# Where the next group's rows are turned, in a fused attention, Fourier mixing and expert kernel: six edits of order

## The chip, the cores and the metric

The kernel runs on one core of one Trainium2 chip. The metric is device microseconds of one execution. Three runs of the kernel before took 918.91, 921.63 and 917.93 us, so their median is 918.91 us. The profiled execution took 917.5 us, of which its trace spans 915.7 us.

Five engines run at the same time, each through a list of instructions in its own order: TensorE (PE in the rows, its weight loads PEld), VectorE (DVE), ScalarE (ACT), GpSimd (POOL) and SyncE (SP), which here only issues DMAs. An instruction that waits for another engine holds up what stands behind it in its own list.

## The reference, cut to what matters

Three layers follow each other, for 4 batches of 576 tokens with 512 features:

```python
# 1. attention, 8 heads of 64, window of 128, causal, a linear bias per head
attn = softmax(where(mask, scale * q @ k.T + bias, -1e9));  x = attn @ v     # (B, S, 512)
# 2. Fourier mixing, then a two-layer product on normalised rows
u  = x + real(fft(fft(x, axis=1), axis=2))
un = (u - mean(u)) / sqrt(var(u) + 1e-6)
x2 = u + maximum(un @ w_ch1, 0) @ w_ch2                                      # hidden width 2048
# 3. one expert of 8 per token; some tokens keep the expert of the token before
logits = x2 @ w_gate;   keep = sigmoid(x2 @ w_local) >= 0.5
out[s] = softmax(logits[s])[e] * (maximum(x2[s] @ w1[e], 0) @ w2[e])         # e chosen token by token
```

## The kernel before

**Tiles and precision.** The 2304 tokens are 18 tiles of 128 rows. Nine groups of two tiles go through layer 2. Large products are made of three TensorE products on numbers split in a high and a low part (`mm3`: high weights times high input, high weights times low input, low weights times high input). `split` makes the parts: ScalarE copies the high part, VectorE subtracts it from the source to get the low part.

**A pass of layer 2.** The hidden width is done in two halves. `mlp_first` runs the first half for the nine groups while attention and mixing of later batches still go on; the second half runs after all of them. A pass of `ffn` over one group has eight hidden blocks. Block f takes 12 products into the tile `hps` (lines 184 to 186), ScalarE takes the maximum with zero (line 732), VectorE makes its low part (line 735), and then 6 products add block f-1 into `acc` (lines 754 and 758). `ffn` yields after each of these pieces: piece 0 is block 0's `hps`, piece 2f-1 is block f's `hps`, piece 2f is `acc` of block f-1, piece 15 the last `acc`. So pieces 11 and 13 are the `hps` of blocks 6 and 7, and pieces 12, 14 and 15 the `acc` of blocks 5, 6 and 7.

**Preparation of the next group.** Between the pieces of group j, `normalise` prepares group j+1 one step at a time, behind the pieces that the table `STEPS` names: ask for the rows (0), statistics (3), the reciprocal root on GpSimd (5), scaling of both tiles on ScalarE into `u` (10, line 875), then `transpose_split` of each tile (13 and 15): four TensorE transposes into `tps` (line 704), a ScalarE cast into the high part of `xT` (line 180), a VectorE subtraction into its low part (line 181), and a store of `xT` for the second half (line 880, SyncE). Group j+1's first product reads the high part of both tiles, its second one the low part. Where the rows are not mixed yet, the preparation begins later, at piece 5 or when they are. After a pass, ScalarE copies both `acc` tiles out and stores them (lines 916 and 917). Group 0 has its own table, `STEPS0`.

**Attention.** `attention` takes the ten units of a batch through four parts: `scores` and a row minimum, `exps` on ScalarE, `flip` (four transposes, tile `pt`, and the mask on GpSimd), `values` (products into `o`, copied to `ot`, lines 459 to 467), and `natural` (transposes of `ot` into `xps`, line 479, then a reciprocal and a product on VectorE into `x`). Units are staggered: in step u the parts work on units u, u-1, u-2, u-3 and u-4. From batch 1 on, a step yields twice, and `natural` of unit u-4 stands at the head of the step.

**What sets the order.** The opening (batch 0 and the first normalisation) is written out by hand. After it, `run` picks the next piece from lanes (attention, mixing, layer 2, weight conversion) by their due positions, and a scheduler sets each engine's order from there. PSUM tiles of the small parts (`pt`, `o`, `xps`, `tps`, `zps`) share three buffers.

**The router.** In the second half, `route` makes the logits of a group with eight products of 256 columns (line 1220): for each of the four feature blocks, one with the high part of `x2T` and one with its low part.

Of the kernel before, what the change touches and what calls it, by code (L numbers as in the profile page):

```python
# [65 lines left out]
VL = 3  # L66
NP = 5

STEPS = (0, 3, 5, 10, 13, 15)
STEPS0 = (9, 11, 12, 13, 14, 15)  # L70

QK = 2 * (HALF + 33)
# [100 lines left out]
def build(ctx, tc, a, out):  # L173
# [161 lines left out]
    def load_part(b, g, part):  # L335

        t = qk.tile([P, 2, QK], F32, tag="qk", name="qkt")
        nc.sync.dma_start(out=t, in_=a["qk"][b, g, part])
        return t, load_values(b, g, part)
# [50 lines left out]
    def attention(b, between=None):  # L390
# [103 lines left out]
        for u in range(len(units) + VL + 1):  # L494
            if ahead < 4 and u in (0, 2, 5):
                g, p = parts[ahead]
                R[g, p] = load_part(b, g, p)
                ahead += 1
            if b == 1 and u == 6:
                three = slab([P, 2, K1 + 1], F32, "three", "m", MB)  # L500
                nc.sync.dma_start(out=three, in_=a["three"])
            if b == 1 and u == 10:
                nc.scalar.copy(tab3, three)
                nc.gpsimd.tensor_tensor(out=tab3[32:64], in0=three[32:64], in1=tab3[32:64].bitcast(F32), op=ALU.subtract)
            if u < len(units) and b == 0:
                scores(u)
            if b == 0 and u == FL:
                flip(0)
            if 1 <= u < len(units) + 1:
                exps(u - 1)  # L510
            if b:
                if VL < u:
                    natural(u - VL - 1)
                if FL <= u < len(units) + FL:
                    flip(u - FL)
                yield
                if u < len(units):
                    scores(u)
                if VL <= u < len(units) + VL:
                    values(u - VL)  # L520
                yield
                continue
            yield

            def fill():
                if b == 0 and u >= len(units) - 1:
                    spin(SPIN_)

            def back():
                if VL < u:  # L530
                    natural(u - VL - 1)

            def weights():
                if FL <= u < len(units) + FL:
                    if b or u > FL:
                        flip(u - FL)
                    fill()

            def mean():
                if VL <= u < len(units) + VL:  # L540
                    values(u - VL)
                    fill()

            part = (back, weights, mean)
            if b == 0:
                part = {len(units): (mean, weights, back), len(units) + 1: (back, weights, between, mean), len(units) + 2: (mean, back)}.get(u, part)
            for p in part:
                p()
            yield
# [264 lines left out]
    def normalise(gs, xT, j, src=None):  # L814
        n = len(gs)
        mv = sm2.tile([P, TM, 2], F32, tag="mv", name="mv")
        st = sm2.tile([P, TM, 6], F32, tag="st", name="st")
        later = src is None
        if later:
            if j not in rows_of:  # L820
                ask_rows(j)
            src = rows_of[j]
        yield
        for i in range(n):
            nc.vector.bn_stats(st[:, i], src[i])
            if i + 1 < n and not later:
                yield
        for i in range(n):
            nc.vector.bn_aggr(mv[:, i], st[:, i])
        yield  # L830

        v = sm2.tile([P, 3, TM], F32, tag="v", name="v")
        v0, v1, v2 = (v[:, i, 0:n] for i in range(3))

        eng = nc.gpsimd if later else nc.vector
        eng.tensor_scalar_add(v0, mv[:, 0:n, 1], 1.0e-6)
        if later:
            nc.gpsimd.tensor_tensor(out=v1, in0=v0, in1=half[:, 0:n], op=ALU.pow)
            for _ in range(2):
                eng.tensor_tensor(out=v2, in0=v1, in1=v1, op=ALU.mult)  # L840
                eng.tensor_tensor(out=v2, in0=v2, in1=v0, op=ALU.mult)
                eng.tensor_scalar(out=v2, in0=v2, scalar1=-0.5, scalar2=1.5, op0=ALU.mult, op1=ALU.add)
                eng.tensor_tensor(out=v1, in0=v2, in1=v1, op=ALU.mult)
            eng.tensor_tensor(out=v2, in0=mv[:, 0:n, 0], in1=v1, op=ALU.mult)
            eng.tensor_scalar_mul(v2, v2, -1.0)
        else:

            nc.gpsimd.tensor_tensor(out=v1, in0=v0, in1=half[:, 0:n], op=ALU.pow)
            eng.tensor_scalar_mul(v0, v0, -0.5)
            for _ in range(2):  # L850
                eng.tensor_tensor(out=v2, in0=v1, in1=v1, op=ALU.mult)
                eng.tensor_tensor(out=v2, in0=v2, in1=v0, op=ALU.mult)
                eng.scalar_tensor_tensor(out=v1, in0=v2, scalar=1.5, in1=v1, op0=ALU.add, op1=ALU.mult)
            last["v"] = eng.scalar_tensor_tensor(out=v2, in0=mv[:, 0:n, 0], scalar=-1.0, in1=v1, op0=ALU.mult, op1=ALU.mult)
        yield
        if not later:
            us = []
            for i in range(n):
                us.append(act.tile([P, DM], F32, tag="u", name="u", bufs=UB))
                if i:  # L860
                    nc.vector.tensor_scalar(out=us[i], in0=src[i], scalar1=v[:, 1, i:i + 1], scalar2=v[:, 2, i:i + 1], op0=ALU.mult, op1=ALU.add)
                else:
                    nc.scalar.activation(us[i], src[i], AF.Identity, scale=v[:, 1, i:i + 1], bias=v[:, 2, i:i + 1])
            yield
            for i, g in enumerate(gs):
                transpose_split(xT, i * P, us[i])
            for i, g in enumerate(gs):
                nc.sync.dma_start(out=nd[g], in_=xT[:, :, :, i * P:(i + 1) * P].bitcast(F32))
            yield
            return  # L870
        us = []
        with behind():
            for i in range(n):
                us.append(act.tile([P, DM], F32, tag="u", name="u", bufs=UB))
                nc.scalar.activation(us[i], src[i], AF.Identity, scale=v[:, 1, i:i + 1], bias=v[:, 2, i:i + 1])
        yield
        for i, g in enumerate(gs):
            with behind():
                transpose_split(xT, i * P, us[i])
            nc.sync.dma_start(out=nd[g], in_=xT[:, :, :, i * P:(i + 1) * P].bitcast(F32))  # L880
            yield
# [9 lines left out]
    def prepare(j, src=None):  # L891
        xT = act.tile([P, 2, 4, TM * P], F32R, tag="xT", name="xT")
        ph[j] = xT
        return normalise(GA[j], xT, j, src)

    def mlp_first():

        need = [0, 0, 1, 1, 2, 2, 3, 3, 3]
        for j, gs in enumerate(GA):
            xT = ph.pop(j)  # L900
            acc = []
            pre = None
            done = 0
            steps = STEPS if j else STEPS0
            for n, _ in enumerate(ffn(xT, len(gs) * P, chunksA, banks, acc, hidden, (ps_a, ps_a))):
                if j + 1 < len(GA) and done < len(steps) and n >= steps[done]:
                    if pre is None and (n >= NP or mixed[0] >= need[j + 1]):
                        yield ("need", lambda: mixed[0] >= need[j + 1])
                        pre = prepare(j + 1)
                    if pre is not None:  # L910
                        next(pre)
                        done += 1
                yield ("piece", 1)
            for i, g in enumerate(gs):
                y = act.tile([P, DM], F32, tag="y", name="y")
                nc.scalar.copy(y, acc[i])
                nc.scalar.dma_start(out=pd[g], in_=y)
            if pre is not None:
                for _ in pre:
                    yield ("piece", 0)  # L920
# [292 lines left out]
    def route(gs, xT, apart, late_copy):  # L1213
        n = len(gs) * P
        ng = len(gs)
        ps = ps_g.tile([P, DM], F32, tag="g", name="lps")
        r2 = 2 * (E + 2)
        for k in range(4):
            for j in range(2):
                nc.tensor.matmul(ps[0:r2, 0:n], lhsT=wg[:, k].rearrange("p h e -> p (h e)"), rhs=xT[:, j, k, 0:n],  # L1220
                                 start=k == 0 and j == 0, stop=k == 3 and j == 1)
        lt = lact.tile([r2, TM * P], F32, tag="lt", name="lt", bufs=1)
# [462 lines left out]
    with tc.If(most > 0):  # L1685
        for r in range(E):
            n = nc.values_load(eid[0:1, 3, r:r + 1], min_val=0, max_val=-(-(NT - CAPS[r]) // P))
# [54 lines left out]
```

## Time and profile before

| | |
|---|---|
| median of three runs | 918.91 us (917.93 to 921.63) |
| profiled execution | 917.5 us, trace 915.7 us |
| TensorE busy | 877.0 us, 96% of the span |
| VectorE, ScalarE, GpSimd busy | 527.5, 385.0 and 220.4 us |
| first halves of the nine groups | about 62 to 416 us of the span |
| mean granted clock of TensorE | 0.991 |

Starts are counted from the trace's first instruction. A row of the timeline gives start and length in us, engine, source line, operation, tile written, tiles read, shape and how many equal instructions follow each other; in brackets stands how long the engine was idle before it and which engine and line ended that. A TensorE instruction counts as busy while it is in the pipe, so that the next one starts before it ends.

### The profile page before, as it was taken

How to read it: one execution, taken by the hardware profiler on the slowest of the kernel's cores; microseconds unless marked ns; L12 is line 12 of the kernel's file. 1: busy time of each engine (PE TensorE's matmuls, PEld its weight loads, DVE VectorE, ACT ScalarE, POOL GpSimd, SP SyncE). 2: the span in 40 equal slices, each digit the busy share in tenths (PEclk: the TensorE clock that was granted, in tenths of full speed). 3: DMA queues.
4: the chain of work that ended last, by engine and by line, in shares of the span. 5: the costliest groups of instructions: out<-in, count | busy, mean ns of one | idle time of the engine just before them, and what ended most of it. 6: DMA issues, size and time to landing. Idle time of an engine off the chain costs nothing. (4 is left out here: it accounts for less than half of the span.)

```text
span 915.7 us, 16165 instructions
## 1 busy us (share of the span) xinstructions
PE 877.0 (96%) x5919; PEld 740.9 (81%) x5919; DVE 527.5 (58%) x1360; ACT 385.0 (42%) x1012; POOL 220.4 (24%) x351
## 2 busy tenths in 40 slices
PE   8987999999999999999999999999999999999993
PEld 5665777778788889889888898888888889888882
DVE  6889957785766687111334535366955655556410
ACT  5756664654553364211122121114534655545311
POOL 2433421431321331010111322223130321122100
PEclk9998999999999999999999999999999999999997
DMA  9942432451405881263444552347735765455100
GB/s 325 384 160 64 152 131 70 146 155 42 151 2 161 259 273 51 69 161 70 116 115 115 104 113 42 102 103 214 217 97 184 255 215 176 153 184 180 69 21 22
DMA packets 103743, 128.75 MB, mean 141 GB/s; under 512 B 10704, under 2 KB 72400, under 8 KB 103622
## 3 DMA queue, kind: packets, MB, share of 16 engines
q1 hardware_dynamic: 78246, 103.54, 34.9%
q0 software_dynamic: 22720, 19.36, 9.5%
q10 hardware_dynamic: 2688, 4.73, 1.4%
q8 instruction: 49, 0.80, 0.3%
q14 instruction: 40, 0.33, 0.1%
HBM read 99.24 MB, written 30.19 MB: 141 GB/s over the span
## 5 line engine op out<-in xcount | busy, mean ns | idle before, releaser
L754 PE MATMUL acc<-t,h 128*128 128x512 f32 x608 | 175.2, 406 | 1.0 <-ACT t L180 1.0
L732 ACT ACTIVATE h<-hps 128x256 fp32r<-128x256 f32 x152 | 58.3, 383 | 267.6 <-PE hps L186 266.8
L735 DVE SCALAR_TENSOR_TENSOR h<-hps,h 128x256 fp32r<-128x256 f32 x152 | 63.8, 420 | 137.3 <-ACT h L732 135.9
L754 PEld LDWEIGHTS acc<-t,h 128*128 128x128 f32 x608 | 105.3, 190 | 19.2 <-issue 1.9
L181 DVE TENSOR_TENSOR t<-we,t 128x512 fp32r<-128x512 f32 x128 | 84.2, 687 | 36.7 <-ACT t L180 34.0
L758 PE MATMUL acc<-t,h 128*128 128x512 f32 x304 | 95.6, 396 | 0.4 <-DVE h L735 0.4
L184 PE MATMUL hps<-xT,t 128*128 128x256 f32 x288 | 84.4, 295 | 5.6 <-ACT xT L180 3.5
L180 ACT CAST t<-we 128x512 fp32r<-128x512 f32 x128 | 74.3, 618 | 27.1 <-PE acc L758 22.1
L185 PE MATMUL hps<-xT,t 128*128 128x256 f32 x288 | 82.6, 287 | 1.5 <-DVE xT L181 1.5
L184 PE MATMUL hps<-xTb,t 128*128 128x256 f32 x288 | 83.9, 291 | 0.0
L184 PE MATMUL hps<-xTe,t 128*128 128x256 f32 (+6 forms) x288 | 83.5, 290 | 0.0
L185 PE MATMUL hps<-xTe,t 128*128 128x256 f32 (+6 forms) x288 | 83.0, 288 | 0.0
L186 PE MATMUL hps<-xTe,t 128*128 128x256 f32 (+6 forms) x288 | 82.9, 288 | 0.0
L186 PE MATMUL hps<-xT,t 128*128 128x256 f32 x288 | 82.1, 286 | 0.0
L186 PE MATMUL hps<-xTb,t 128*128 128x256 f32 x288 | 81.4, 283 | 0.0
L185 PE MATMUL hps<-xTb,t 128*128 128x256 f32 x288 | 81.4, 283 | 0.0
L431 ACT ACTIVATE t<-t,mx 128x128 f32<-128x128 f32 (+1 forms) x160 | 62.4, 392 | 29.0 <-DVE mx L424 25.8
L754 PE MATMUL acc<-t,hE 128*128 128x512 f32 (+3 forms) x256 | 70.9, 399 | 0.3 <-ACT hE L732 0.3
L758 PEld LDWEIGHTS acc<-t,h 128*128 128x128 f32 x304 | 56.8, 189 | 13.8 <-DVE h L735 1.1
L184 PEld LDWEIGHTS hps<-xT,t 128*128 128x128 f32 x288 | 55.0, 192 | 12.2 <-ACT xT L180 4.6
L735 DVE SCALAR_TENSOR_TENSOR hE<-hps,hE 128x256 fp32r<-128x256 f32 (+3 forms) x96 | 29.7, 338 | 59.9 <-ACT hE L732 57.8
L185 PEld LDWEIGHTS hps<-xT,t 128*128 128x128 f32 x288 | 55.4, 192 | 4.1 <-DVE xT L181 2.3
(327 smaller groups left out, 1857.2 us busy)
## 6 DMA issues: line engine op xcount, KB each, us to landing
we<-in_w SPq DMA_DIRECT2D x64, 512.0 KB
rw<-in_w_ch SPq DMA_DIRECT2D x32, 512.0 KB
qkt<-in_qk SPq DMA_DIRECT2D x15, 642.0 KB
nd<-xT SPq DMA_DIRECT2D x18, 512.0 KB
xTb<-nd POOLq DMA_DIRECT2D x18, 512.0 KB
vt<-in_v SPq DMA_DIRECT2D x16, 384.0 KB
pd<-y ACTq DMA_DIRECT2D x18, 256.0 KB
ub<-ud SPq DMA_DIRECT2D x18, 256.0 KB
```

The source lines that it names most:

```text
L180: last["hi"] = nc.scalar.copy(hi, src)
L181: return (eng or nc.vector).tensor_tensor(out=lo, in0=src, in1=hi.bitcast(F32), op=ALU.subtract)
L184: nc.tensor.matmul(o, lhsT=wh, rhs=xh, start=start, stop=False, **kw)
L185: nc.tensor.matmul(o, lhsT=wh, rhs=xl, start=False, stop=False, **kw)
L186: return nc.tensor.matmul(o, lhsT=wl, rhs=xh, start=False, stop=stop, **kw)
L431: nc.scalar.activation(t[0:m, j], t[0:m, j], AF.Exp, bias=mx[0:m, j:j + 1], scale=-1.0, accum_out=sums[0:m, j:j + 1])
L732: last["relu"] = nc.scalar.activation(h[:, 0:n], hps[:, 0:n], AF.Relu)
L735: last["rest"] = nc.vector.scalar_tensor_tensor(out=h[:, lo:lo + c1 - c0], in0=hps[:, c0:c1], scalar=0.0, in1=h[:, c0:c1].bitcast(F32), op ...
L754: nc.tensor.matmul(acc[t][0:m], lhsT=h[:, c:c + m], rhs=t2[:, j, g % per], start=g == 0 and j == 0, stop=False)
L758: last["acc"] = nc.tensor.matmul(o, lhsT=x, rhs=t2[:, j, g % per], start=first_ and j == 0, stop=g == nf - 1 and j == js[-1])
```

## The change

There are six edits of order; the number of instructions of each kind stays the same. Transposes of the next group's rows stand behind pieces 11 and 13 instead of 13 and 15. Where the preparation began late, a new table puts them behind 13 and 14. In batches 1 to 3, `natural` goes from the head of a step to its end. In the opening, VectorE scales tile 0 and ScalarE tile 1 instead of the other way round. In the router, all four products with high parts stand ahead of the four with low parts.

```diff
-STEPS = (0, 3, 5, 10, 13, 15)
+STEPS = (0, 3, 5, 10, 11, 13)
+LATE = (0, 3, 5, 10, 13, 14)
 STEPS0 = (9, 11, 12, 13, 14, 15)
...
             if b:
-                if VL < u:
-                    natural(u - VL - 1)
                 if FL <= u < len(units) + FL:
                     flip(u - FL)
                 yield
...
                 if VL <= u < len(units) + VL:
                     values(u - VL)
+                if VL < u:
+                    natural(u - VL - 1)
                 yield
...
-                if i:
+                if not i:
                     nc.vector.tensor_scalar(out=us[i], in0=src[i], ...)
                 else:
                     nc.scalar.activation(us[i], src[i], AF.Identity, ...)
...
                         pre = prepare(j + 1)
+                        if j and n > 0:
+                            steps = LATE
...
-        for k in range(4):
-            for j in range(2):
+        for j in range(2):
+            for k in range(4):
                 nc.tensor.matmul(ps[0:r2, 0:n], lhsT=wg[:, k]..., rhs=xT[:, j, k, 0:n], ...)
```

In the orders below, a row is source line, operation, tile written, tiles read, shape and count. Line numbers of the changed file are one to three higher than before for the same statement (704 is 705, 916 is 919).

TensorE before, at the end of the first half of group 7, before group 8 begins; `t_1173` and `t_787` are weights of the last and first hidden blocks, `t_1257` the second layer's for the last two:

```order
L186 MATMUL hps<-xT,t_1173 128x256
L704 MATMUL tps<-ident,u 128x128 x4
L754 MATMUL acc<-t_1257,h 128x512 x4
L758 MATMUL acc<-t_1257,h 128x512 x2
L754 MATMUL acc<-t_1257,h 128x512 x4
L758 MATMUL acc<-t_1257,h 128x512 x2
L704 MATMUL tps<-ident,u 128x128 x4
L184 MATMUL hps<-xT,t_787 128x256 x2
L185 MATMUL hps<-xT,t_787 128x256
```

TensorE of the changed kernel at the same place:

```order
L187 MATMUL hps<-xT,t_1173 128x256
L705 MATMUL tps<-ident,u 128x128 x4
L755 MATMUL acc<-t_1257,h 128x512 x4
L759 MATMUL acc<-t_1257,h 128x512 x2
L755 MATMUL acc<-t_1257,h 128x512 x4
L759 MATMUL acc<-t_1257,h 128x512 x2
L185 MATMUL hps<-xT,t_787 128x256
L186 MATMUL hps<-xT,t_787 128x256
```

Tile 1's transposes moved from behind the two last `acc` pieces to ahead of them; tile 0's, which stood there, moved up by one block (they stand behind block 6's `hps`, 15 rows further up).

ScalarE before, over the same pass; `u` are the scaled rows, `h` the hidden block, `y` the `acc` copies:

```order
L875 ACTIVATE u<-r,v 128x512 x2
L732 ACTIVATE h<-hps 128x256 x2
L180 CAST xT<-tps 128x4x128
L916 COPY y<-acc 128x512
L180 CAST xT<-tps 128x4x128
L917 DMA pd_92<-y 128x512
L916 COPY y<-acc 128x512
```

ScalarE of the changed kernel over the same pass:

```order
L876 ACTIVATE u<-r,v 128x512 x2
L733 ACTIVATE h<-hps 128x256
L181 CAST xT<-tps 128x4x128
L733 ACTIVATE h<-hps 128x256
L181 CAST xT<-tps 128x4x128
L919 COPY y<-acc 128x512 x2
```

Tile 1's cast stood behind the first copy of the finished pass, and now stands right behind the last hidden block, with tile 0's cast ahead of that block.

TensorE before, in batch 2's attention beside the first half of group 1 (about 182 to 186 us of the trace):

```order
L459 MATMUL o<-w,vt 64x128 x7
L754 MATMUL acc<-t_1112,h 128x512 x4
L758 MATMUL acc<-t_1112,h 128x512 x2
L479 MATMUL xps<-ident,ot 128x128 x2
L440 MATMUL pt<-ident,t 128x128 x4
```

TensorE of the changed kernel at that place:

```order
L460 MATMUL o<-w,vt 64x128 x8
L480 MATMUL xps<-ident,ot 128x128 x2
L755 MATMUL acc<-t_1112,h 128x512 x4
L759 MATMUL acc<-t_1112,h 128x512 x2
L441 MATMUL pt<-ident,t 128x128 x4
```

The two transposes of `ot` before take the unit whose `o` products stand right above them; in the changed kernel they take the unit before that one.

## Rows read from the trace of the kernel before

**Rows 1.** Busy time by stretch: stretch, its length, engines' busy us, granted clock, DMA

```profile
60.00:105.00 45.00, 38.85 (x247) 28.62 (x248) 43.81 (x77) 28.62 (x82) 14.43 (x15) 0.92 0.37 117
76.00:83.00 7.00, 6.36 (x21) 4.87 (x21) 7.00 (x15) 3.64 (x10) 1.82 (x2) 0.51 0.08 20
105.00:312.00 207.00, 202.52 (x1564) 164.50 (x1563) 143.31 (x347) 107.10 (x357) 57.99 (x147) 1.00 0.36 115
312.00:417.00 105.00, 100.05 (x633) 89.14 (x633) 53.19 (x107) 43.10 (x88) 21.16 (x33) 1.00 0.50 154
```

**Rows 2.** Waits of TensorE, whole span: waited for, us in total, times, longest

```profile
PE hps L184 <- ACT xT L180: 3.5, 4, 1.2
PE pt L440 <- ACT t L431: 3.3, 4, 1.2
PE xps L479 <- ACT ot L467: 1.6, 2, 1.2
...
PE hps L185 <- DVE xT L181: 1.5, 4, 0.8
...
PE tps L704 <- ACT u L863: 0.8, 1, 0.8
...
PE lps L1220 <- DVE x2T L181: 0.7, 1, 0.7
```

**Rows 3.** Timeline, TensorE, from group 4's pass to group 5's

```profile
312.07 0.60 PE L704 MATMUL tps<-ident,u 128*128 128x128 f32 x4
312.43 1.18 PE L754 MATMUL acc<-t,h 128*128 128x512 f32 x4
...
315.27 0.60 PE L704 MATMUL tps<-ident,u 128*128 128x128 f32 x4
317.06 0.50 PE L184 MATMUL hps<-xT,t 128*128 128x256 f32 x2 [1.19 <-ACT xT L180]
...
317.79 0.39 PE L185 MATMUL hps<-xT,t 128*128 128x256 f32 x1 [0.22 <-DVE xT L181]
```

**Rows 4.** Timeline, TensorE, from group 5's pass to group 6's

```profile
340.88 0.49 PE L704 MATMUL tps<-ident,u 128*128 128x128 f32 x3
342.21 0.51 PE L184 MATMUL hps<-xT,t 128*128 128x256 f32 x2 [0.84 <-ACT xT L180]
...
343.51 0.38 PE L185 MATMUL hps<-xT,t 128*128 128x256 f32 x1 [0.79 <-DVE xT L181]
```

**Rows 5.** Timeline, all engines, from group 7's pass to group 8's

```profile
388.56 2.09 POOL L1531 DMA_DIRECT2D xTb<-nd  x2 [42.33 <-PE hps L186]
...
389.33 0.69 DVE L181 TENSOR_TENSOR xT<-tps,xT 128x512 fp32r<-128x512 f32 x1 [0.21 <-ACT xT L180]
...
391.27 0.60 PE L704 MATMUL tps<-ident,u 128*128 128x128 f32 x4
391.47 0.59 ACT L916 COPY y<-acc 128x512 f32<-128x512 f32 x1 [2.17 <-PE acc L758]
...
391.95 0.59 ACT L180 CAST xT<-tps 128x512 fp32r<-128x512 f32 x1
...
392.60 0.50 PE L184 MATMUL hps<-xT,t 128*128 128x256 f32 x2 [0.73 <-ACT xT L180]
...
393.32 0.39 PE L185 MATMUL hps<-xT,t 128*128 128x256 f32 x1 [0.22 <-DVE xT L181]
```

**Rows 6.** Timeline, ScalarE and TensorE, in batch 2's attention

```profile
184.78 0.36 ACT L465 COPY ot<-o 128x256 f32<-128x256 f32 x1
...
185.19 0.44 PE L479 MATMUL xps<-ident,ot 128*128 128x128 f32 x2 [0.90 <-ACT ot L465]
```

**Rows 7.** Timeline, ScalarE, VectorE and TensorE, in the opening's normalisation

```profile
59.03 0.81 ACT L863 ACTIVATE u<-x,v 128x512 f32<-128x512 f32 x1 [0.47 <-DVE v L854]
...
59.03 0.55 DVE L861 TENSOR_SCALAR u<-x,v 128x512 f32<-128x512 f32 x1
...
59.90 1.09 PE L704 MATMUL tps<-ident,u 128*128 128x128 f32 x8 [0.78 <-ACT u L863]
```

## The prediction
> **What bounds the kernel now.** I read the views in this order: busy time by stretch, TensorE's waits, then the timeline at the longest of them.
>
> The table by stretch shows who sets the time where the change acts [rows 1]. From 312 to 417 us, when attention and mixing are over and layer 2's first half runs alone, TensorE is busy 100.05 of 105 us, so only its own 4.95 us of waits can be taken from it. From 105 to 312 us it idles 4.5 of 207 us; of the other engines VectorE works most, 143 us. From 60 to 105 us the picture differs: VectorE is busy 43.8 of 45 us with the weight conversion and TensorE 38.9. There a reordering of TensorE's list gains little, because what it waits for is late anyway.
>
> The waits say what the 4.95 us are [rows 2]. The first product of a pass waits 3.5 us in 4 cases for the high part of `xT`, and the second kind of product 1.5 us in 4 cases for its low part: 5.0 us, four of each. The timeline shows that these are the four last changes of group [rows 3 to 5] (the one from group 6 to 7 repeats the pattern of the last). The earlier ones show no such wait, since attention and mixing have products to put in between.
>
> What happens at such a change is seen best at the last one [rows 5]. Tile 1's transposes start at 391.27, as the last thing of the pass. ScalarE then first takes up a copy of the finished `acc` (391.47), then the cast (391.95); TensorE starts the new pass at 392.60 and stops again until VectorE has made the low part (393.32). The chain is transposes, cast, subtraction, and nothing lies beside it.
>
> **The change part by part.**
>
> *Row transposes.* Nothing is added or removed: 8 transposes, 2 casts, 2 subtractions and 2 stores per group are issued earlier. I price the wait at the four changes by starts. Where nothing is late, the product behind four transposes starts 0.36 us after the first of them (312.07 to 312.43) [rows 3]. Where the chain ends last it starts 1.79 us after it (315.27 to 317.06) [rows 3], and 1.33 us after it in the three others (340.88 to 342.21, 391.27 to 392.60) [rows 4, 5]. That is 1.43 + 3 x 0.97 = 4.3 us. The second stop adds the 1.5 us of idle time for the low parts [rows 2]. Together 5.8 us.
>
> Does the new place hide the chain? The row that shows it is in the same trace: tile 0's transposes stand, before the change, exactly where tile 1's stand after it, behind block 7's `hps`. From there to the end of the last `acc` piece it is 3.2 us (312.07 to 315.27) [rows 3]. In the last such pass tile 0's low part was done at 389.33 + 0.69 = 390.0, 1.2 us before that end at 391.27 [rows 5]. Tile 0 itself moves up by one block more. What is late next is a plain hidden block. ScalarE's cast now stands ahead of block 7's maximum, but tile 0's cast did not hold up `acc` where it stood. The two copies of `acc` (0.59 us each) now come right at the end of the pass; the next writer of `acc` comes only after two `hps` blocks. Bounds: 5.0 us, the idle time alone [rows 2], and 7.8 us, if the whole of the restart between first and third product (0.73 + 1.30 + 2 x 0.72 = 3.5 us) went [rows 3 to 5]. I take 5.8, nearest to the starts that rows show.
>
> The Trainium skill (Perfetto Trace Analysis, "Tensor Engine Instruction (MATMUL, LD_WEIGHTS)") says that the end of a TensorE instruction in the profile is estimated, not observed. By that, the idle column understates a stop and starts are the safer measure; by the idle column this term would be 5.0, and by starts it is what I took.
>
> The stores of `xT` pass other loads on SyncE's list, and on GpSimd's list one addition for the second half now stands ahead of the load that was issued at 388.56 [rows 5]. The loaded tile is needed when the next pass is over, and a pass takes 25.1 us (317.06 to 342.21) [rows 3, 4]; a delay of a few us there is covered, so I price it at nothing.
>
> *Attended rows last.* Before, the transposes of a unit's result stand right behind the products that make it, with ScalarE's copy in between: at 185.19 TensorE has stood for 0.90 us because the copy ran from 184.78, behind that unit's exponentials [rows 6]. In the changed order a unit's flip, scores and the next unit's values lie between. These waits are 1.6 us (copy of line 467) and 0.90 us [rows 2, 6], 2.5 us at most. The change only moves where in a step TensorE meets ScalarE, and other waits may come instead; the nearest row is the flip's wait for exponentials, 3.3 us in 4 cases [rows 2]. So this term lies between +2.5 and -3.3. I take 1.5, because in the new order the distance grows for every unit, while nothing else in a step gets closer.
>
> *First rows on VectorE.* Both engines start scaling at 59.03; ScalarE takes 0.81 us, VectorE 0.55, and the transposes of tile 0 wait for ScalarE's tile [rows 7]. After the swap tile 0 is ready 0.26 us earlier and tile 1 when tile 0 was, when TensorE is still busy with tile 0's transposes. I take 0.26; the bounds are -0.25 (two score products that ran before the wait now come behind it) and the 0.78 us of the wait.
>
> *Logits' high parts first.* One wait of 0.7 us for the low part of `x2T` stands in the whole second half [rows 2]. Three more products now run ahead of the first that needs it. Bounds 0 and 0.7; I take 0.35, since the low part's VectorE chain itself is not moved.
>
> The sum is 5.8 + 1.5 + 0.26 + 0.35 = 7.9 us. The profiled execution took 917.5 us, so 909.6. The median of the runs is 918.9, 1.4 above the profiled execution; on that scale I predict 911.0. The terms' bounds, with the attention term not below zero, give this case a range of its own of 907 to 914.
>
> **The rivals.**
>
> *Attention gives its part back.* The waits on `ot` go, and the flips or the values products wait instead, at the -3.3 us of the bound. In favour: from 60 to 105 us VectorE has 1.2 us free in 45 [rows 1], so a unit's later reciprocal and product delay something there. Against: from 105 us on VectorE has 64 us free. The time: 5.8 - 3.3 + 0.6 = 3.1 us gained, 915.8.
>
> *The slow clock stretch goes.* From 76 to 83 us TensorE's granted clock is 0.51, its lower level (1.2 of 2.4 GHz), after waits of up to 1.2 us for exponentials [rows 1, 2]. At half rate 7 us hold 3.4 us of loss. If the moved transposes of `ot` close enough of those waits, the clock stays up and the kernel takes 907.6. Against: the order of TensorE's list up to the first of those waits is nearly as before, and VectorE is the bound there, so I expect the stretch to remain. The Trainium skill (TensorE: Matmul & The Clock Gate, "HAM oscillation — how this bites in real kernels") has the clock fall back after waits and cost half of the slow time; the trace agrees with 0.51 granted after the waits.
>
> *`natural` holds a shared PSUM buffer longer.* This one is slower. `xps` now comes behind `values`, and its buffer, one of three, is free only when VectorE has multiplied. If the next flip, score step or row transpose then has to wait for it, that happens in each of the 30 units of batches 1 to 3. It decides from 0.26 us a unit (7.9 / 30). With 0.5 us each, less than the 0.90 us that one wait on `ot` cost, it is 15 us: 7 slower, 926. Against: the three buffers go round in the same cycle of `pt`, `o`, `xps` as before, and from 105 us on VectorE is busy for only 69% of the time.
>
> *The row chain still ends last.* In the passes at 312 to 367 us weight conversion also fills ScalarE and VectorE, and the change from group 5 to 6 has the longest second stop, 0.79 us [rows 4]. If casts queue behind conversions by the 2 to 3 us that the new place gives, the 5.8 us stay, and the time is 916.8. Against it: the changed ScalarE order has tile 1's cast right behind the last hidden block.
>
> **How the numbers follow.** The forecast has 0.62, attention giving back 0.17, the clock stretch going 0.12, the row chain still last 0.05, the held buffer 0.04. A measurement of this kernel tells about 0.5% from no change, 4.6 us, so faster means below 914.3. Faster: nearly all of the forecast (0.61), the clock case (0.12) and a fifth of attention giving back (0.03), 0.76. Within 0.5%: the rest of that, the chain still last and the forecast's edge, 0.20. Slower: the held buffer, 0.04. The range reaches from 904.5, the forecast's lower end with most of the clock's 3.4 us, to 916.5, which takes in attention giving back; beyond it lie most of the chain case and the held buffer.
>
> **What would show it.** At the four last changes of group, the first `hps` product starts within half a microsecond of the last `acc` product, and TensorE's rows for waits on `xT` are gone or below 1 us. From 312 to 417 us (less the shift) TensorE idles under 1 us. The rows for waits on `ot` in batches 1 to 3 fall below 1 us in sum, and no row for flips, `o` or `tps` grows by as much. The opening's transposes start 0.26 us earlier against VectorE's last scalar step. The granted clock still has one stretch near 0.5 between 70 and 90 us. The prediction is wrong if the passes alone still show 5 us of waits, or if TensorE's idle time between 60 and 312 us grows by over 2 us.

## The result and the profile after

The changed kernel takes 912.34 us (median of 6 runs, 911.24 to 912.87) against 919.5 us before (6 runs, 917.34 to 924.39): 0.9916 of the time, 95% interval 0.9894 to 0.9937. Run again beside other kernels it took 912.78 us against 919.02, 0.9929 (0.9909 to 0.9949). The prediction was 911.0 us. Its profiled execution took 912.26 us, of which the trace spans 910.5; for the whole execution the prediction's sum had said 909.6.

Busy time by stretch, after (columns as in [rows 1]; the second stretch is chosen around the clock's dip):

```profile
60.00:105.00 45.00, 37.08 (x244) 27.37 (x244) 43.98 (x77) 28.91 (x81) 14.56 (x14) 0.96 0.34 103
76.00:84.00 8.00, 6.33 (x27) 4.70 (x29) 8.00 (x16) 4.63 (x15) 1.82 (x2) 0.79 0.20 50
105.00:312.00 207.00, 202.20 (x1562) 163.56 (x1561) 141.17 (x348) 106.91 (x359) 55.55 (x143) 1.00 0.36 117
312.00:417.00 105.00, 104.11 (x671) 94.08 (x670) 55.04 (x112) 44.13 (x91) 22.65 (x38) 1.00 0.55 166
```

From 312 to 417 us TensorE's idle time went from 4.95 us [rows 1] to 0.89. From 105 to 312 us it grew, from 4.48 to 4.80 us.

TensorE's waits, after, whole span:

```profile
PE pt L441 <- ACT t L432: 3.9, 4, 1.9
...
PE acc L759 <- DVE h L736: 1.3, 3, 0.5
...
PE hps L185 <- DVE h L736: 1.2, 2, 0.8
PE tps L705 <- DVE u L862: 1.0, 1, 1.0
PE pc L602 <- DVE xT L182: 1.0, 1, 1.0
PE xps L480 <- ACT w L445: 0.9, 1, 0.9
...
PE s L420 <- DVE t L424: 0.8, 1, 0.8
...
PE pt L441 <- DVE x L488: 0.6, 1, 0.6
...
PE pt L441 <- ACT ot L468: 0.4, 1, 0.4
```

The eight waits of `hps` on `xT` are gone, and so is the wait of the logits. The waits of `xps` on `ot` in batches 1 to 3 are gone too, but other rows stand in their place: `xps` on the mask copy `w`, `pt` on `x` and on `ot`, `hps` on the hidden block's low part, `s` on `t`, `pc` on mixing's `xT`. Three of them are no waits for data, since `xps` reads `ident` and `ot`, and `pt` reads `ident` and `t`. The copies `w`, `x` and `ot` empty `pt`, `xps` and `o`, which share three PSUM buffers, so by the program TensorE waits there for a buffer.

The change from group 4's pass to group 5's, after, TensorE, ScalarE and VectorE (answers to [rows 3]):

```profile
313.95 0.60 PE L705 MATMUL tps<-ident,u 128*128 128x128 f32 x4
...
314.31 1.17 PE L755 MATMUL acc<-t,h 128*128 128x512 f32 x4
314.59 0.59 ACT L181 CAST xT<-tps 128x512 fp32r<-128x512 f32 x1
...
315.70 0.68 DVE L182 TENSOR_TENSOR xT<-tps,xT 128x512 fp32r<-128x512 f32 x1
...
316.69 0.61 PE L759 MATMUL acc<-t,h 128*128 128x512 f32 x2
317.14 0.28 PE L185 MATMUL hps<-xT,t 128*128 128x256 f32 x1
317.26 0.28 PE L186 MATMUL hps<-xT,t 128*128 128x256 f32 x1
...
317.34 1.08 ACT L919 COPY y<-acc 128x512 f32<-128x512 f32 x2
```

Tile 1's transposes start at 313.95, the low part is done at 315.70 + 0.68 = 316.38, and the new pass begins at 317.14 with no idle time: 0.76 us to spare. At the last change (answers to [rows 5]) 1.24 us are to spare (387.19 + 0.69 to 389.12):

```profile
385.93 0.60 PE L705 MATMUL tps<-ident,u 128*128 128x128 f32 x4
...
387.19 0.69 DVE L182 TENSOR_TENSOR xT<-tps,xT 128x512 fp32r<-128x512 f32 x1 [0.22 <-ACT xT L181]
...
388.67 0.61 PE L759 MATMUL acc<-t,h 128*128 128x512 f32 x2
389.12 0.28 PE L185 MATMUL hps<-xT,t 128*128 128x256 f32 x1
```

In batch 2's attention (answers to [rows 6]) TensorE no longer waits for `ot`; the transposes of `ot` now wait as long, 0.93 us, for ScalarE's copy of another unit's `pt` into its mask tile `w`, which frees a shared buffer:

```profile
189.94 0.56 ACT L445 COPY w<-pt 128x512 f32<-128x512 f32 x1
...
190.55 0.44 PE L480 MATMUL xps<-ident,ot 128*128 128x128 f32 x2 [0.93 <-ACT w L445]
```

In the opening (answers to [rows 7]) the scaling starts at 60.38 on both engines, and the transposes wait for VectorE's tile alone and begin 0.69 us after that start instead of 0.87. TensorE's idle time ahead of them is longer than before, 1.02 us against 0.78, since four score products that ran there now come behind them:

```profile
60.38 0.81 ACT L864 ACTIVATE u<-x,v 128x512 f32<-128x512 f32 x1 [0.48 <-DVE v L855]
60.38 0.55 DVE L862 TENSOR_SCALAR u<-x,v 128x512 f32<-128x512 f32 x1
...
61.07 1.06 PE L705 MATMUL tps<-ident,u 128*128 128x128 f32 x8 [1.02 <-DVE u L862]
```

**Where the time went, by fixed points.** Waits move between rows and engines; the time between two fixed points of TensorE's own list doesn't. For every kernel below I took from the trace the start of the first score product, the start of the opening's transposes, and the end (start plus length) of the last `acc` row of a pass; the last column runs from the end of group 8's first half to the end of the last second-half pass. In us:

| kernel | first score product starts | from it to opening's transposes | from these to end of group 4's pass | of it group 1's pass | end of group 4's to end of group 8's | second half's nine passes |
|---|---|---|---|---|---|---|
| before | 6.32 | 53.58 | 255.53 | 75.98 | 100.46 | 235.10 |
| after | 7.66 | 53.41 | 256.24 | 79.08 | 94.52 | 233.75 |
| after, again | 6.24 | 53.39 | 256.23 | 79.16 | 94.52 | 234.49 |
| steps_only | 6.60 | 53.57 | 255.07 | 76.44 | 95.30 | 237.51 |
| steps_13_14 | 6.79 | 53.57 | 254.84 | 76.41 | 96.39 | 234.91 |
| attended_only | 7.56 | 53.57 | 257.06 | 79.10 | 100.34 | 234.88 |
| all_but_attended | 6.66 | 53.40 | 255.27 | 76.43 | 94.59 | 234.36 |
| attended_mid | 7.19 | 53.38 | 255.00 | 76.10 | 95.63 | 233.99 |
| no_late | 6.62 | 53.40 | 257.33 | 78.37 | 95.10 | 235.05 |
| small_only | 6.13 | 53.40 | 255.45 | 75.96 | 103.58 | 234.09 |

The row transposes' share of after is 100.46 - 94.52 = 5.94 us. From the opening to group 4 the changed kernel loses 0.7 us, and 1.34 us more because its first score product came later in that execution, which its second profile doesn't repeat. The second half's nine passes are 1.35 us shorter, 0.61 in the second profile. From their end to the last `acc` product it takes 250.1 to 250.2 us in every kernel but no_late (251.2), and from there to the end 14.5 to 14.8 us, so the table leaves both out.

### The profile page after: what moved, and what is told of

Same layout as the page of the kernel before. It is cut to its first block, busy times and chain, and to the rows that moved or that the text cites. A ratio compares the mean times of both kernels' runs of the same rounds, so it can differ in the third digit from the quotient of the medians.

```text
span 910.5 us, 16176 instructions
## 1 busy us (share of the span) xinstructions
PE 875.2 (96%) x5919; PEld 739.9 (81%) x5919; DVE 524.4 (58%) x1360; ACT 384.1 (42%) x1012; POOL 219.1 (24%) x351
## 4 chain that ended last, share of the span: by engine, by line
PE 74%; DVE 10%; issue 6%; ACT 4%; DMA 3%; POOL 2%; POOLq 0%; DVEq 0%; ACTq 0%
PE acc L755 18%; PE acc L759 11%; PE hps L185 10%; PE hps L186 10%; PE hps L187 10%; PE o L460 2%; PE tps L705 2%; PE s L420 2%; PE zps L674 2%; ACT t L432 2%; DVE t L310 1%; PE xps L480 1%; PE pt L441 1%; DVE t L311 1%; PE lps L1223 1%
## 5 line engine op out<-in xcount | busy, mean ns | idle before, releaser
L185 PEld LDWEIGHTS hps<-xT,t 128*128 128x128 f32 x288 | 55.3, 192 | 7.7 <-DVE h L736 2.6
L185 PEld LDWEIGHTS hps<-xTe,t 128*128 128x128 f32 x288 | 54.6, 189 | 3.4
```

Of the source, the lines that this page charges most:

```text
L185: nc.tensor.matmul(o, lhsT=wh, rhs=xh, start=start, stop=False, **kw)
```

## The experiments

**Only the row transposes (steps_only).** The kernel before with the two tables alone:

```diff
-STEPS = (0, 3, 5, 10, 13, 15)
+STEPS = (0, 3, 5, 10, 11, 13)
+LATE = (0, 3, 5, 10, 13, 14)
+                        if j and n > 0:
+                            steps = LATE
```

> The kernel before with only the two tables of steps changed (transposes behind pieces 11 and 13, or 13 and 14 where preparation begins late). Theory, that the chain transposes, cast, subtraction ended the wait at the four last changes of group and the other edits gave almost nothing: the stretch from group 4's end to group 8's end is 5.9 us shorter, the time is 5 to 6.5 us less, ratio 0.993 to 0.9945. Rival, that the attended rows gave the rest of the measured 7.2 us: ratio 0.994 or above here, and the missing 1.5 to 2 us show in the next kernel.

Measured: 912.74 us (909.77 to 916.12, 7 runs) against 919.37, ratio 0.992 (0.9891 to 0.995). The four changes of group give 100.46 - 95.30 = 5.16 us in this execution (0.51 of the difference to after is one late hidden block right after a change of group, on ScalarE). The two tables alone give what the whole change gives, within the interval.

**Only the attended rows last (attended_only).** The kernel before with one edit:

```diff
             if b:
-                if VL < u:
-                    natural(u - VL - 1)
...
                     values(u - VL)
+                if VL < u:
+                    natural(u - VL - 1)
                 yield
```

> The kernel before with only `natural` moved to the end of a step. Theory, that the waits on `ot` go but other waits on ScalarE and VectorE take their place: ratio 0.999 to 1.002, waits on `ot` in batches 1 to 3 near zero, TensorE's time from the opening's transposes to the end of group 4's pass the same within 1 us. Rival, my prediction's term: 1.5 us less, ratio 0.9984 or below.

Measured: 922.02 us (917.26 to 926.44, 12 runs), ratio 1.0022 (1.0 to 1.0044): no gain. By fixed points it loses 257.06 - 255.53 = 1.53 us, with group 1's pass 3.1 us longer and the passes around it taking part of that back. That is more than the 1 us that the theory allowed, and the rival, 1.5 us less, fails. Its TensorE waits between 105 and 312 us:

```profile
PE pc L601 <- DVE xT L181: 1.1, 1, 1.1
PE xps L479 <- ACT w L444: 0.9, 1, 0.9
PE s L419 <- DVE t L423: 0.8, 1, 0.8
...
PE hps L184 <- DVE h L735: 0.4, 1, 0.4
```

**All but the attended rows (all_but_attended).** The changed kernel with `natural` back at the head of the step:

```diff
             if b:
+                if VL < u:
+                    natural(u - VL - 1)
...
-                if VL < u:
-                    natural(u - VL - 1)
                 yield
```

> The changed kernel with `natural` back at the head of a step. Theory: 6 to 7 us less than the kernel before, ratio 0.9925 to 0.9935, so as fast as the changed kernel or up to 1 us faster. Rival, that attended rows last earns 1.5 us together with the other edits: ratio 0.9932 or above and 1.5 us slower than the changed kernel.

Measured: 912.3 us (910.92 to 916.82, 6 runs), ratio 0.992 (0.9889 to 0.9951). The median can't tell it from after. The fixed points can: 255.27 us from the opening to group 4's end against 256.24 and 256.23 in the two profiles of after, and 76.43 us for group 1's pass against 79.08 and 79.16. The edit costs about 1 us.

**Half the way for one tile (steps_13_14).** The kernel before with tile 1's transposes one `acc` piece earlier:

```diff
-STEPS = (0, 3, 5, 10, 13, 15)
+STEPS = (0, 3, 5, 10, 13, 14)
```

> The kernel before with tile 0's transposes left behind piece 13 and tile 1's moved from 15 to 14. One `acc` piece (about 1.4 us) then stands behind tile 1's transposes. Theory, that the chain of about 2 us counts against what stands behind it: at the last changes of group the wait shrinks by 1.1 to 1.4 us but some tenths stay for the low part, 4 to 5.5 us of the 5.9 gained, ratio 0.994 to 0.996. Rival, that two pieces of cover are needed or that tile 0 matters as much: under 3 us gained, ratio over 0.997.

Measured: 913.87 us (912.97 to 915.8, 7 runs), ratio 0.9929 (0.9905 to 0.9954); the four changes give 100.46 - 96.39 = 4.07 us. The kernel gains more than the ratio of 0.994 that was expected, and not by the expected way: three changes show no wait for `xT` at all, and the one from group 5 to 6 has all that is left, 1.88 us. Its timeline, TensorE, ScalarE and VectorE, without the hidden block's rows:

```profile
337.23 0.60 PE L704 MATMUL tps<-ident,u 128*128 128x128 f32 x4
...
338.03 0.57 ACT L180 CAST xT<-tps 128x512 fp32r<-128x512 f32 x1
...
338.46 0.69 DVE L309 SCALAR_TENSOR_TENSOR t<-rw 128x512 uint32<-128x512 uint32 x1
...
340.60 0.69 DVE L181 TENSOR_TENSOR xT<-tps,xT 128x512 fp32r<-128x512 f32 x1
...
341.34 0.39 PE L185 MATMUL hps<-xT,t 128*128 128x256 f32 x1 [1.88 <-DVE xT L181]
```

The cast ends at 338.60, but the subtraction begins at 340.60: VectorE has taken up the conversion of weights at 338.46, four instructions of it. So the rival "the row chain still ends last" has a real mechanism. It decides with one `acc` piece of cover, in one change out of four; with two pieces no profile here shows a wait for `xT` at the last four changes.

**The changed kernel once more (after_again).** No edit.

> The changed kernel once more, unaltered, to see what of its one profile repeats. Theory A (moving the attended rows costs TensorE time in group 1's pass, between 118 and 194 us): from the end of group 0's pass to the end of group 1's it again takes about 79 us against 76 us where only that edit is left out, and about 256 us from the opening's transposes to the end of group 4's pass. Rival (that difference is one execution's chance): 76 to 77 us and about 255 us. The first score product started 1.2 us later in both profiles that have the attended rows last (7.6 against 6.3 to 6.6 us): if that belongs to the program it comes again, if it is the first loads' landing in one execution it comes out anywhere from 6.3 to 7.7 us. Time by both 911 to 914 us; the slow clock stretch near 79 us between 3.4 and 6.8 us long.

Measured: 912.78 us (911.01 to 914.36, 6 runs). Group 1's pass takes 79.16 us again and the stretch to group 4's end 256.23: the loss belongs to the program. The first score product starts at 6.24 us, against 7.66: that does not. Over ten profiles it starts between 6.13 and 7.66 us, and the two ends of nearly that whole range belong to one program, so the start is a property of the execution. The clock is told below.

**The attended rows in the middle (attended_mid).** The changed kernel with `natural` behind the flip:

```diff
                     flip(u - FL)
+                if VL < u:
+                    natural(u - VL - 1)
                 yield
...
                     values(u - VL)
-                if VL < u:
-                    natural(u - VL - 1)
                 yield
```

> The changed kernel with the attended rows' transposes one place earlier: behind the unit's flip, ahead of the yield, instead of behind scores and values. Theory A (the loss comes from the place at the step's end, where the transposes pile onto scores and values and TensorE then meets ScalarE's copies and VectorE's hidden blocks late): the waits on `ot` stay away because four flip transposes lie between, the new waits at 187 to 191 us (0.40 and 0.93 us) go, group 1's pass takes 76 to 77 us and the stretch from the opening to the end of group 4's pass 255 us or less; time about 910.5 us. Theory B (the waits only move with any order, their sum is set by ScalarE's and VectorE's chains): waits between 105 and 312 us again near 5 us, group 1's pass 78 to 80 us, time about 912.5 us. Rival C (the transposes right behind the flip wait for a PSUM buffer of three, since `pt` must first be copied): new waits of `o` or `xps` on VectorE's product or ScalarE's mask copy, time 914 us or more.

Measured: 912.02 us (910.49 to 914.66, 6 runs), ratio 0.9921 (0.99 to 0.9943). Group 1's pass takes 76.10 us and the opening to group 4's end 255.00, the shortest but one of all. Theory A holds on the place, B's 78 to 80 us and C's 914 us fail. Two of A's signs did not come: waits on `ot` are back, 1.1 us for `xps`, and the time is not 910.5 us. Its waits between 105 and 312 us, the three largest:

```profile
PE xps L480 <- ACT cmb L606: 1.0, 1, 1.0
PE xps L480 <- ACT ot L468: 0.6, 1, 0.6
PE pc L602 <- DVE xT L182: 0.5, 1, 0.5
```

All of that view's rows sum to 3.5 us here, 3.9 in after_again, 4.2 in attended_only and 4.0 before, while group 1's pass differs by 3 us. The sums hide it because the window is wider than the pass: before's 4.0 us hold a wait of 1.2 us for `ot` in group 0's pass, which went, and other waits came in group 1's. These are busy times of group 1's pass alone (columns as in [rows 1]), of before, attended_only, all_but_attended, after and attended_mid:

```profile
117.94:193.92 75.98, 74.03 (x600) 56.98 (x599) 56.80 (x135) 41.91 (x153) 26.69 (x63) 1.00 0.39 127
118.05:197.15 79.10, 75.39 (x605) 57.28 (x603) 54.56 (x134) 42.37 (x153) 26.98 (x66) 1.00 0.39 122
118.05:194.48 76.43, 74.51 (x605) 57.40 (x603) 56.84 (x131) 42.42 (x154) 26.65 (x64) 1.00 0.40 131
117.89:196.97 79.08, 75.82 (x608) 57.76 (x607) 55.25 (x135) 42.87 (x154) 26.99 (x66) 1.00 0.41 128
118.46:194.56 76.10, 74.33 (x604) 56.94 (x605) 56.16 (x134) 42.63 (x154) 27.62 (x66) 1.00 0.41 129
```

TensorE is idle for 1.95 us there before, 1.92 in all_but_attended and 1.77 here, but for 3.71 in attended_only and 3.26 in after. So idle time holds 1.3 to 1.8 us of the 2.65 to 3.1 us by which the attended rows at the step's end lengthen the pass; between the kernels compared the number of products differs by five at most. What this kernel gains up to group 4's end against after (256.24 - 255.00 = 1.24 us) it loses behind it in this execution (95.63 - 94.52 = 1.11 us), where `acc` waits 0.6 us for a late hidden block. On time it is a tie with after; nothing run here is measurably faster than after.

**Without the second table (no_late).** The kernel all_but_attended with:

```diff
-LATE = (0, 3, 5, 10, 13, 14)
+LATE = STEPS
```

> The changed kernel without the attended edit, and with the table LATE equal to STEPS, so that row transposes stand behind pieces 11 and 13 also where the preparation began late. Theory A (LATE keeps TensorE from meeting scaled rows that are not ready yet): in group 1's to group 3's passes the `tps` transposes then wait for ScalarE's `u`, 0.5 to 1.5 us more in sum, time 913 to 914 us. Rival (attention's products fill that place anyway, as no wait on `xT` or `u` stands there in any run so far): no new wait on `u` or `xT`, within 0.5 us of the kernel with LATE in TensorE's time from the opening to the end of group 4's pass, time 912 to 913 us.

Measured: 914.42 us (910.67 to 915.29, 6 runs), ratio 0.9937 (0.9915 to 0.996). From the opening to group 4's end it takes 257.33 us, 2.06 more than with LATE. It begins at one row in TensorE's timeline:

```profile
182.17 0.72 PE L705 MATMUL tps<-ident,u 128*128 128x128 f32 x4 [1.65 <-ACT u L876]
```

Right behind that stop the granted clock falls (columns as in [rows 1]), while in all_but_attended it stays at 1.00 in both windows:

```profile
181.00:185.00 4.00, 2.83 (x14) 1.77 (x16) 0.93 (x3) 3.70 (x13) 1.38 (x5) 0.70 0.42 126
185.00:189.00 4.00, 4.00 (x33) 3.55 (x34) 3.03 (x6) 1.19 (x3) 0.21 (x1) 0.87 0.76 248
```

The transposes stand ahead of the point at which ScalarE has the scaled rows. Theory A holds: the second table keeps 2 us that the first alone would give away. How much of that is the stop and how much the clock behind it, one profile does not separate.

**Only the two small edits (small_only).** The kernel before with:

```diff
-                if i:
+                if not i:
                     nc.vector.tensor_scalar(out=us[i], in0=src[i], ...)
...
-        for k in range(4):
-            for j in range(2):
+        for j in range(2):
+            for k in range(4):
```

> Only the first rows on VectorE and the logits' high parts first; everything else as before. Priced at 0.26 and 0.35 us: TensorE's opening transposes wait for VectorE's `u` and the wait for the low part of `x2T` (0.7 us before) is gone, 918.2 to 918.7 us on the scale of the median 919.4. Rival (both are worth nothing, because the opening's VectorE chain just starts the next thing later and the logits' wait comes back at the next product): the same 919.4 us, group 0's pass unchanged at 58 us and the second half unchanged at 235.1 and 250.2 us. Both are far below what a median tells, so TensorE's time by stretch decides.

Measured: 919.32 us (917.14 to 923.09, 12 runs), ratio 0.9994 (0.9979 to 1.001). The opening's transposes come 0.18 us earlier after the first score product (53.40 against 53.58), in every profile with the edit. The logits now run as one group of eight, and a wait comes back behind them, as `acc`'s for the low part of a hidden block:

```profile
630.89 1.08 PE L1220 MATMUL lps<-x2T,wg 128*20 128x256 f32 x8
...
640.32 0.74 PE L758 MATMUL acc<-t,h 128*128 128x512 f32 x2 [0.98 <-DVE h L735]
```

At that place before waited 0.37 us, so 0.69 + 0.37 = 1.06 us became 0.98 (after: 0.35 + 0.53 = 0.88; its second profile: 0.73 + 0.58 = 1.31). The place itself gains next to nothing in these. The second half's nine passes are shorter all the same: 233.75 to 234.49 us in five profiles with the edit against 234.88 to 235.10 in three without it (steps_only left out, whose clock dropped there), but 235.05 in no_late, which has it too. Their means, 234.3 with all six and 235.0, differ by 0.7 us. Pass by pass, about 0.3 us of this is steady: the second, third, fourth, sixth and eighth pass take 0.04 to 0.10 us less each in all six profiles with the edit, no_late included, than in those without it, though nothing waited at their logits. In before's second pass it is 2.65 us from the first logits product to the next hidden block's first, here 2.60. The fifth, seventh and ninth pass scatter, 79.5 to 79.7 us together without the edit and 78.6 to 80.0 with it. So the rival (worth nothing) fails for the opening and, by 0.3 us, for the logits; on the median the two together are not to be seen.

## Why the prediction was right or wrong

**Row transposes: right, mechanism and size.** Predicted 5.8 us from starts, measured 5.94 in both profiles of after. The four other kernels with these places give 4.8 to 5.9 us; where it is least, in attended_mid, TensorE waits for a hidden block right behind the first of the changes. TensorE's idle time from 312 to 417 us fell by only 4.06 us, so starts were the better measure than the idle column. All signs named for it came: the new passes begin 0.45 us after the last `acc` row's start, the waits on `xT` are gone, the stretch idles 0.89 us. What this term left out is LATE: the text priced the four last changes and said nothing of the late preparations. Run without the second table, the kernel loses 2.06 us there.

**Attended rows last: wrong in sign.** This is the step that failed. It took 1.5 us of gain "because in the new order the distance grows for every unit, while nothing else in a step gets closer". The measured term is a loss of 1.0 us (after against all_but_attended) to 1.5 us (attended_only against before), so 2.5 to 3.0 us off. The waits of `xps` on `ot` did go, so the distance did grow. But something else did get closer: at the step's end the transposes stand behind scores and values, and TensorE waits for ScalarE's mask copy (0.93 us), which frees a shared buffer, and for VectorE's hidden block and `t`. In group 1's pass alone its idle time grew by 1.3 to 1.8 us. The rival "attention gives its part back" described this and had 0.17; its price, 3.3 us lost, was too high. Placed behind the flip the same transposes cost nothing (attended_mid). Why the pass is 1.3 us longer still, beyond its idle time, stays open.

**First rows on VectorE: right.** Predicted 0.26 us, measured 0.18, which is kept: from the first score product to the end of group 0's pass before takes 53.58 + 58.04 = 111.62 us and small_only 53.40 + 57.99 = 111.39.

**Logits: right in sign, by another way.** Predicted 0.35 us within 0 to 0.7, for the end of one wait. The wait did go, but in the profiles compared most of it came back at the next `acc`. The steady gain, 0.3 us, lies in five other passes that had no such wait; that its size is near the prediction's is luck. The rest of the 0.7 us between the means lies in passes that scatter as much.

**The clock stretch: its price was wrong.** The rival had 3.4 us for it. In after the granted clock from 76 to 84 us is 0.79, so about half of the slow stretch did go; in after_again it is 0.57, as before. These are after_again's rows for two stretches:

```profile
60.00:105.00 45.00, 39.38 (x250) 28.65 (x248) 44.02 (x77) 29.11 (x84) 14.80 (x15) 0.92 0.39 124
76.00:84.00 8.00, 7.36 (x29) 5.33 (x28) 8.00 (x17) 4.64 (x11) 1.82 (x2) 0.57 0.07 18
```

From the opening's transposes to the end of group 0's pass after takes 56.82 us and after_again 56.92. Half a slow stretch is worth 0.1 us there, because VectorE is busy for 8.00 of the 8 us in both: a faster TensorE only waits more (busy 37.08 against 39.38 of 45 us). The Trainium skill (TensorE: Matmul & The Clock Gate, "HAM oscillation — how this bites in real kernels") prices throttled time at half of it; the runs here show that only where TensorE is the bound (the two passes of small_only in the last section). For the same reason a sign of the prediction misled: idle time from 60 to 312 us grew by 2.1 us (10.63 to 12.72), over the bound of 2 us named, while after_again, the same program, shows 10.28.

**Held buffer: its mechanism is seen, but not in every unit.** In after `pt` waits 0.6 us for the product `x`, which frees the buffer of `xps`. Two more waits are for a shared buffer, that of `xps` on `w` (0.93 us) and that of `pt` on `ot` (0.4), so 1.9 us in all. The rival had 0.5 us for each of 30 units; the size of one wait was right, the number was not. Against it the prediction had said that the buffers go round in the same cycle; that did not keep these waits away.

**The sum.** 5.94 - 1.0 + 0.18 + 0.7 = 5.8 us, against 7.9 predicted; the 2.1 us between are the attended rows' 2.5 less the logits' 0.35. From the first score product to the end of the ninth second-half pass the table gives 6.8 us for after and 6.0 for its second profile. The medians differ by 7.2 and 6.2 us, each uncertain by about 2 us (0.0022 of 919), so they hold both sums. Part of the medians' difference goes with the clock. Of the 36 executions of the kernel before that ran beside the other kernels, 17 have a mean granted clock of 0.988 or less and a median of 921.15 us, and the 19 others have 918.61. The 12 of the changed kernel all have 0.989 or more and a median of 912.44, 6.2 us below those 19. That the predicted time was met within 1.4 us is in part luck: a term 2.5 us too high was in the sum, and the prediction had no term for the clock at the changes of group.

## What to carry to other kernels

Preparation of the next pass belongs one piece further ahead than its own chain needs, since another engine's queue can add to the chain in one pass and not in others; but where its input is late, the same early place turns into a wait of its own. A wait that vanishes from a list of waits is not yet a gain: take the engine's time between two fixed points of its own list, before and after, and sum waits between the same two points. Before pricing a slow clock or an idle column, look which engine is busy all of that stretch.

## What the runs showed of the hardware

The clock also dropped in places where before's profile shows none, in single executions. In small_only the granted clock fell after the stops at two changes of group (1.37 + 0.23 us and 0.84 + 0.79 us), to 0.57 in each of these windows:

```profile
318.00:322.00 4.00, 4.00 (x23) 3.96 (x22) 0.64 (x4) 0.44 (x2) 0.00 (x0) 0.57 1.00 336
345.00:349.00 4.00, 4.00 (x23) 4.00 (x22) 2.32 (x6) 0.38 (x1) 2.26 (x3) 0.57 0.78 254
```

Here TensorE is busy all the time, and the four passes take 103.58 - 100.46 = 3.1 us longer, all of it in the two with a drop. Before had nearly the same stops (1.19 + 0.22 and 0.84 + 0.79 us [rows 3, 4]) and no drop. In steps_only the clock fell the same way after a stop of 1.76 us in the logits at 625.7 us, and the second half's nine passes took 2.4 us longer than before's; steps_13_14 has a stop of 1.68 us at the same place, and its clock stayed at 1.00. So a stop at a change of pass costs more in some executions than its own length. The mean granted clock of each execution suggests that the row transposes' edit also keeps the clock up in more of them: 31 of the 60 executions of before, attended_only and small_only have 0.988 or less, and 1 of the 44 of the six kernels with moved row transposes. Where it fell in those 31 is known for small_only's profile alone.
